# Two-stage attention and two feed-forward layers on one core: a transfer, the maxima, the weighted sums and the last results reordered

## The chip, the cores and the metric

The kernel runs on one core of a Trainium2 chip. The metric is the device time of one execution in microseconds (us). The engines are TensorE (PE, its weight loads PEld), VectorE (DVE), ScalarE (ACT), GpSimd (POOL) and SyncE (SP), which issues all the DMAs. Each engine takes its instructions in the order in which the program writes them.

## The reference, cut to what matters

```python
def sm_attn(qq, kk, vv):
    s = scale * np.matmul(qq, kk.transpose(0, 1, 3, 2))
    s = s - np.max(s, axis=-1, keepdims=True)
    a = np.exp(s)
    a = a / (np.sum(a, axis=-1, keepdims=True) + 1e-09)
    return np.matmul(a, vv)
p_packed = sm_attn(p, k, v)
out = sm_attn(q, p_packed, p_packed)      # 4 batches, 8 heads, 576 rows, 64 columns
x = out with its heads side by side       # 2304 x 512
x = softplus(x @ w_in) @ w_out            # 512 -> 2048 -> 512, in float32
return silu(x @ w_in2) @ w_out2
```

## The kernel before, in words

The schedule is written out by hand: the order in which the program emits instructions is each engine's order. A piece of work is a Python generator (`Item`) that yields the name of the point at which its next part is due. `run_steps` walks through 128 steps; `go(point)` runs the parts of the step's items that are due at that point. A step `s` goes: "next", "D0", "A0"; `emit_in(s)`, six matmuls that make one 128x288 block `h` of the hidden layer; "PE"; `emit_out(s)`, the matmuls of an output block `y` (in step 2 it stands ahead of `emit_in`); `act_scalar`, the softplus; "A1", "D1", "A2"; `act_vector`, the low part of the softplus; "D" and `finish_out`, which adds `y` to the sum `ya` (in steps 4 to 7 it stands ahead of "D"); then the step's loads. A point beginning with D holds VectorE work, with A ScalarE work, and "PE" TensorE work.

For batch `b`, with t = 8b, the items are:

- `att1(b)` packs the values: `scores` (L324, into two tiles of PSUM), maxima `top` (L330, L331, VectorE), `exp` (L337), transposes `turn` (L346), copies `turned` (L350, L353, ScalarE), weighted sums `weigh` (L361, 80 small matmuls), normalising (L386 to L389, VectorE), a transpose (L394) and its copy `pt` (L398). For b > 1 its parts stand in steps t-10, t-9, t-7, t-6 and t-5, so the scores of batch 2 are in step 6 and those of batch 3 in step 14.
- `att2(2b)` and `att2(2b+1)` are the second attention for 288 columns each: scores (L409, one PSUM tile), a transpose on VectorE (L418), maximum, subtraction (L420, L421), exponential (L423, ScalarE), then at point D0 sum, reciprocal, product and transpose (L425 to L430), and the split into `ax` (L435 ScalarE, L437 VectorE), which `emit_in` (L488) reads.
- `packed(b, qs)` multiplies the packed values with two chunks of the first weight (L454, one PSUM tile), copies the high part `vw` on ScalarE (L462) and subtracts for the low part on VectorE (L466, which reads the PSUM tile again). `packed(b, (0,))` stands in step 8b-4 and `packed(b, (1,))` in step 8b-3, that is 5, 13 and 21.

All of these tiles come from `two_banks()`, a pool with two buffers (`psa`), each of two PSUM banks. Four more banks hold `h` and `y`.

Weights come as 64-bit numbers. A chunk is loaded (L128), scaled on ScalarE (L140) and put together on VectorE (L152, L159); some are then split into high and low parts (L171, L173). `start()` writes out by hand what precedes the steps: loads, dummy matmuls `warm(n)` (L680, 2n instructions), batch 0's attention, and the conversion of the weight chunks ("i", 0 to 3) and ("o", 0 to 3) among it.

In `second()` the second layer is made by a Strassen-like scheme. At its end `group_of` makes, for each of the sums Q1, Q4, Q5, Q6, Q7, Q3, Q2 and for two halves d, a block on TensorE (L1008); `add_group` adds it on VectorE (L1023) and joins sums on GpSimd (`gps`, L1024) and VectorE (`vec`), and `send` (L1029) issues the transfer of a finished 128x384 block on SP's queue.

Of the kernel before, what the change touches and what calls it, by code (L numbers as in the profile page):

```python
# [13 lines left out]
ALU = mybir.AluOpType  # L14
# [4 lines left out]
B, H, S, D = 4, 8, 576, 64  # L19
# [7 lines left out]
KC = 5  # L27
# [23 lines left out]
def body(ctx, tc, kT, vv, qT, pT, wi1, wo1, wi2, wo2, out):  # L51
# [259 lines left out]
    def att1(b):  # L311

        HS = S // 2
        sm = l0.tile([P, 8], F32, name="sm", bufs=2)
        e, et, s1 = [None] * NR, [None] * NR, [None] * NR

        def scores():
            pz, kt = kts[b]
            s1[:] = two_banks(), two_banks()
            for half in range(2):  # L320
                for k in range(NK):
                    for r in range(NR):
                        rows = slice(64 * r, 64 * r + 64)
                        nc.tensor.matmul(  # L324
                            s1[r][32 * k:32 * k + 32, half, :HS], lhsT=pz[rows, k, :],
                            rhs=kt[rows, k, half * HS:(half + 1) * HS], start=True, stop=True,
                        )

        def top(r):
            nc.vector.tensor_reduce(out=sm[:, r:r + 1], in_=s1[r][:, :, :HS], axis=AX.XY, op=ALU.max)  # L330
            nc.vector.tensor_scalar(  # L331
                out=sm[:, 2 + r:3 + r], in0=sm[:, r:r + 1], scalar1=-SCALE, scalar2=None, op0=ALU.mult
            )

        def exp(r):
            e[r] = att.tile([P, S], F32, name=f"e{r}")
            nc.scalar.activation(  # L337
                out=e[r].rearrange("p (h s) -> p h s", h=2), in_=s1[r][:, :, :HS],
                func=AF.Exp, scale=SCALE, bias=sm[:, 2 + r:3 + r],
            )  # L340

        def turn(r):
            t = s1[r] = two_banks()
            for c in range(KC):
                n = min(P, S - c * P)
                nc.tensor.transpose(t[:n, c // 4, (c % 4) * P:(c % 4 + 1) * P], e[r][:, c * P:c * P + n], ident)  # L346

        def turned(r):
            et[r] = att.tile([P, KC, P], F32, name="et", bufs=2)
            nc.scalar.activation(  # L350
                out=et[r][:, :4, :], in_=s1[r][:, 0, :].rearrange("p (c f) -> p c f", c=4), func=AF.Copy
            )
            nc.scalar.activation(out=et[r][:64, 4, :], in_=s1[r][:64, 1, :P], func=AF.Copy)  # L353

        def weigh(r):
            vt = vts[b]
            for c in range(KC):
                n = min(P, S - c * P)
                for k in range(NK):
                    h = 2 * k + r  # L360
                    nc.tensor.matmul(  # L361
                        po[32 * k:32 * k + 32, r, :D1], lhsT=et[r][:n, c, 32 * k:32 * k + 32],
                        rhs=vt[:n, c, h * D1:(h + 1) * D1], start=(c == 0), stop=(c == KC - 1),
                    )

        yield "PE"
        scores()
        yield "D"
        top(0)
        top(1)  # L370
        yield "A1"
        exp(0)
        exp(1)
        yield "PE"
        turn(0)
        turn(1)
        yield "A1"
        turned(0)
        turned(1)
        yield "PE"  # L380

        po = two_banks()
        weigh(0)
        weigh(1)
        yield "D"
        nc.vector.tensor_scalar(out=sm[:, 4:6], in0=po[:, :, D], scalar1=1e-9, scalar2=None, op0=ALU.add)  # L386
        nc.vector.reciprocal(out=sm[:, 6:8], in_=sm[:, 4:6])
        px = att.tile([P, NR, D], F32, name="px")
        nc.vector.tensor_tensor(  # L389
            out=px, in0=po[:, :, :D], in1=sm[:, 6:8].unsqueeze(2).to_broadcast([P, NR, D]), op=ALU.mult  # L390
        )
        yield "PE"
        pt_ps = two_banks()[:, 0, :P]
        nc.tensor.transpose(pt_ps, px.rearrange("p r d -> p (r d)"), ident)  # L394
        yield "A1"

        pt = pts[b] = l0.tile([P, P], F32, name="pt", bufs=B)
        nc.scalar.activation(out=pt, in_=pt_ps, func=AF.Copy)  # L398
# [46 lines left out]
    def packed(b, qs):  # L445
        yield "PE"
        t = two_banks()
        wide = len(qs) > 1
        for k in range(NK):
            w = whl["i", 2 * qs[0] + (k if wide else k // 2)]  # L450
            w = w if wide else w[:, (k % 2) * 256:(k % 2 + 1) * 256]
            for r in range(NR):
                rows = slice(64 * r, 64 * r + 64)
                nc.tensor.matmul(  # L454
                    t[32 * k:32 * k + 32, r, :512 if wide else 256], lhsT=pts[b][rows, k * NP:(k + 1) * NP],
                    rhs=w[rows, :], start=True, stop=True,
                )
        yield "A1"
        vs = []
        for i, q in enumerate(qs):  # L460
            v = l0.tile([P, 2, NR, 256], F32R, name="vw", bufs=3)
            nc.scalar.activation(out=v[:, 0], in_=t[:, :, 256 * i:256 * i + 256], func=AF.Copy)  # L462
            vs.append(v)
        yield "D"
        for i, (q, v) in enumerate(zip(qs, vs)):
            nc.vector.tensor_tensor(  # L466
                out=v[:, 1], in0=t[:, :, 256 * i:256 * i + 256], in1=v[:, 0].bitcast(F32), op=ALU.subtract
            )
            vw[b, q] = v
# [149 lines left out]
    def plan_all():  # L619
# [48 lines left out]
            last = b == B - 1  # L668
            plan(Item(att2(2 * b + 1, last)), (t - 3, t - 1, t) + (t + 1,) * last)
        for (b, qs), s in vstep.items():  # L670
            plan(Item(packed(b, qs)), (s,))

    POINTS = "D0", "A0", "PE", "A1", "D1", "A2", "D"

# [11 lines left out]
    def start():  # L686
        load_k(0)
        load_w("i", 0)
        load_w("i", 1)
        load_v(0)  # L690
        load_q(0)
        load_w("o", 0)
        load_w("o", 1)
        a1 = [Item(att1(b)) for b in range(2)]
        a2 = [Item(att2(blk)) for blk in range(2)]
        v = Item(packed(0, (0,)))
        w = {(k, n): Item(conv_w(k, n, True)) for k in "io" for n in range(GJ)}
        warm(12)
        a1[0].run("PE")
        load_q(1)  # L700
        load_k(1)
        for n in 2, 3:
            load_w("i", n)
        for n in 2, 3:
            load_w("o", n)
        w["i", 0].run("A0", "D1")
        a1[0].run("D")
        w["i", 1].run("A0")
        a1[0].run("A1")
        w["i", 1].run("D1")  # L710
        warm(10)
        a1[0].run("PE", "A1", "D", "PE")
        load_v(1)
        warm(4)
        w["o", 0].run("A0")
        a1[0].run("D")
        w["o", 0].run("D1")
        a1[0].run("PE", "A1")
        a2[0].run("PE")
        v.run("PE")  # L720
        warm(14)
        a2[0].run("D1", "D")
        v.run("A1", "D")
        w["o", 1].run("A0")
        a2[0].run("A1")
        a2[1].run("PE")
        warm(8)
        a2[0].run("D0")
        a2[1].run("D1")
        a1[1].run("PE")  # L730
        a2[0].run("A1", "D")
        w["i", 2].run("A0")
        w["i", 3].run("A0")
        a2[1].run("D")
        w["o", 2].run("A0")
        a2[1].run("A1")
        w["o", 3].run("A0")
        a1[1].run("D", "A1")
        w["o", 1].run("D1")
        a2[1].run("D0")  # L740
        for item, s in (a2[1], 1), (Item(warm_item(10)), 1), (a1[1], 1), (a1[1], 2), (a1[1], 3):
            plan(item, (s,))
        for k, n, ss in ("i", 2, (1,)), ("i", 3, (2,)), ("o", 2, (3,)), ("o", 3, (4,)):
            plan(w[k, n], ss)

        OS = (3, 4), (4, 5), (5, 6), (10, 11)
        for n in range(GJ):
            plan(w["o", n], OS[n])

    def run_steps(end):  # L750
        for s in range(end):
# [14 lines left out]
            h = emit_in(s)  # L766
            go("PE")
            ys = emit_out(s) if ys is None else ys
            r = act_scalar(s, h)
            go("A1")  # L770
            go("D1")
# [8 lines left out]
                finish_out(s, *y)  # L780
            if late:
                go("D")
            for f in loads.get(s, ()):
                f()

# [144 lines left out]
    def second():  # L930
# [88 lines left out]
        def add_group(p, n, y):  # L1019
# [39 lines left out]
            if q == Q1:  # L1059
                gps(a[Q6], a[Q6], a[Q1])  # L1060
                gps(a[Q2], a[Q2], a[Q1])
            elif q == Q6:
                gps(a[Q5], a[Q5], a[Q6])
                gps(a[Q4], a[Q6], a[Q4], ALU.subtract)
            elif q == Q7:
                vec(a[Q4], a[q], a[Q4])
                send(1, 0, a[Q4])
                vec(a[q], a[q], a[Q5])
                send(1, 1, a[q])
            elif q == Q3:  # L1070
                gps(a[q], a[q], a[Q5])
                send(0, 1, a[q])
            elif q == Q2:
                send(0, 0, place(0, 0))

# [325 lines left out]
```

## Time and profile before

| | before |
|---|---|
| median of 3 runs | 743.41 us (743.38 to 743.85) |
| profiled execution, its own time | 744.61 us |
| its span, first to last instruction | 742.8 us |
| PE busy | 730.9 us (98%) |
| DVE busy | 563.7 us (76%) |
| ACT busy | 389.2 us (52%) |
| POOL busy | 161.7 us (22%) |

Busy is the time in which an engine had an instruction of its own running; matmuls are pipelined, so a busy PE also holds matmuls that wait behind each other. Times in rows are us from the start of the span. In a timeline row come the start, the length, the engine and line, the operation, what it writes and reads, the shape, the count of merged instructions, and, in brackets, how long the engine was idle before it and what ended that.

### The profile page before, as it was taken

The numbers are of one execution on the slowest core, as the hardware profiler recorded it, in microseconds if no ns is written. First come the engines' busy times: TensorE is split into PE (matmuls) and PEld (weight loads), VectorE is DVE, ScalarE is ACT, GpSimd is POOL, SyncE is SP. The second block draws the span as 40 slices with busy tenths as digits, with TensorE's granted clock in tenths as the row PEclk, the third lists the DMA queues.
The fourth block names the chain that finished last, engine by engine and source line by source line (L and its number), as shares of the span: only waits on it lengthen the run. The fifth ranks groups of instructions, "written<-read, shape, count | busy, mean of one in ns | idle before, by whom it ended". The sixth has DMA issues, their size and how long they took to land.

```text
span 742.8 us, 13862 instructions
## 1 busy us (share of the span) xinstructions
PE 730.9 (98%) x5404; PEld 697.9 (94%) x5404; DVE 563.7 (76%) x1020; ACT 389.2 (52%) x745; POOL 161.7 (22%) x138
## 2 busy tenths in 40 slices
PE   7999999999999999999999999999999999999997
PEld 6777889999999999999999999999999999999996
DVE  3888887879968897897746685767776976867666
ACT  3667876666555665566535544343354553454340
POOL 0000000000000000000000000000267999876656
PEclk9999999999999999999999999999999999999999
DMA  9965033144463362464349787889999789998932
GB/s 339 347 226 169 19 143 115 57 185 147 162 231 133 150 218 99 169 255 172 155 145 379 297 325 249 333 309 348 358 349 382 269 266 376 343 344 280 310 118 86
DMA packets 64674, 173.73 MB, mean 234 GB/s; under 512 B 5728, under 2 KB 34400, under 8 KB 61280
## 3 DMA queue, kind: packets, MB, share of 16 engines
q1 hardware_dynamic: 64608, 172.85, 65.2%
q8 instruction: 42, 0.69, 0.4%
q14 instruction: 24, 0.20, 0.1%
HBM read 136.65 MB, written 36.18 MB: 233 GB/s over the span
## 4 chain that ended last, share of the span: by engine, by line
PE 82%; DVE 6%; DMA 5%; ACT 4%; issue 1%; SPq 1%; POOL 0%; POOLq 0%; DVEq 0%
PE y L528 25%; PE h L488 13%; PE y L1008 11%; PE y L1112 8%; PE pA L950 6%; PE pB L950 6%; PE pC L950 6%; PE pD L950 3%; PE psa L454 2%; DMA wd<-whl 2%; DMA raw<-wi 2%; DMA wraw<-wo 2%; PE y L521 1%; DVE ya L1023 1%; PE psa L361 1%
## 5 line engine op out<-in xcount | busy, mean ns | idle before, releaser
L528 PE MATMUL y<-gh,w 128*128 128x288 f32 x960 | 212.1, 296 | 0.2 <-DVE ya L543 0.2
L528 PEld LDWEIGHTS y<-gh,w 128*128 128x128 f32 x960 | 160.4, 188 | 13.0 <-issue 5.5
L528 PE MATMUL y<-gl,w 128*128 128x288 f32 x480 | 141.8, 295 | 0.0
L982 POOL TENSOR_TENSOR sums<-c 128x384 f32<-128x384 f32 x13 | 15.6, 1199 | 551.4 <-ACT c L1264 551.4
L488 PE MATMUL h<-ax,vw 128*128 128x288 f32 x768 | 125.2, 298 | 0.8 <-DVE ax L437 0.7
L488 PEld LDWEIGHTS h<-ax,vw 128*128 128x128 f32 x768 | 109.3, 188 | 3.2 <-DVE ax L437 1.2
L1008 PE MATMUL y<-G,w 128*128 128x384 f32 x480 | 93.9, 334 | 0.0
L528 PEld LDWEIGHTS y<-gl,w 128*128 128x128 f32 x480 | 90.2, 188 | 0.5 <-DVE gl L505 0.5
L1112 PE MATMUL y<-G,w 128*128 128x384 f32 x480 | 89.5, 334 | 0.0
L500 ACT ACTIVATE gt<-h 128x288 f32<-128x288 f32 x120 | 48.6, 405 | 68.6 <-PE h L488 64.0
L1008 PEld LDWEIGHTS y<-G,w 128*128 128x128 f32 x480 | 84.1, 188 | 0.2 <-DVE ya L1023 0.2
L1112 PEld LDWEIGHTS y<-G,w 128*128 128x128 f32 x480 | 83.8, 188 | 0.0
L505 DVE TENSOR_TENSOR gl<-gt,gh 128x288 fp32r<-128x288 f32 x120 | 54.2, 451 | 25.2 <-ACT gh L501 24.3
L950 PE MATMUL pA<-xc,w 128*128 128x384 f32 x288 | 57.8, 334 | 0.1
L950 PE MATMUL pB<-xc,w 128*128 128x384 f32 x288 | 57.7, 334 | 0.0
L950 PE MATMUL pC<-xc,w 128*128 128x384 f32 x288 | 57.6, 334 | 0.0
L501 ACT ACTIVATE gh<-gt 128x288 fp32r<-128x288 f32 x120 | 53.4, 445 | 3.8
L545 DVE TENSOR_TENSOR ya<-y,ya 128x288 f32<-128x288 f32 x104 | 46.8, 451 | 7.2 <-PE y L528 7.0
L950 PEld LDWEIGHTS pA<-xc,w 128*128 128x128 f32 x288 | 50.4, 188 | 0.4 <-ACT ta L1182 0.4
L950 PEld LDWEIGHTS pB<-xc,w 128*128 128x128 f32 x288 | 50.6, 188 | 0.0
L1260 ACT ACTIVATE tc<-tc 128x384 f32<-128x384 f32 x24 | 12.6, 526 | 72.4 <-DVE tc L1160 72.3
L990 POOL TENSOR_TENSOR G<-sums,G 128x384 fp32r<-128x384 f32 x40 | 49.0, 1248 | 7.1 <-ACT G L986 7.1
(143 smaller groups left out, 1167.7 us busy)
## 6 DMA issues: line engine op xcount, KB each, us to landing
w<-wd SPq DMA_DIRECT2D x84, 512.0 KB, 6.0
wd<-whl SPq DMA_DIRECT2D x8, 1792.0 KB, 7.1
w<-td SPq DMA_DIRECT2D x56, 256.0 KB, 6.4
w<-od SPq DMA_DIRECT2D x42, 256.0 KB, 5.8
w<-od SPq DMA_DIRECT2D x20, 512.0 KB, 6.6
wraw<-wi SPq DMA_DIRECT2D x16, 512.0 KB, 5.5
wraw<-wo SPq DMA_DIRECT2D x16, 512.0 KB, 6.2
raw<-wi SPq DMA_DIRECT2D x16, 512.0 KB, 6.0
```

Of the source, the lines that this page charges most:

```text
L454: nc.tensor.matmul(t[32 * k:32 * k + 32, r, :512 if wide else 256], lhsT=pts[b][rows, k * NP:(k + 1) * NP], rhs=w[rows, :], start=True, st ...
L488: nc.tensor.matmul(h, lhsT=w, rhs=x, start=(i == 0), stop=(i == len(mm) - 1))
L500: nc.scalar.activation(out=gt, in_=h, func=AF.Softplus)
L501: nc.scalar.activation(out=gh, in_=gt, func=AF.Copy)
L505: nc.vector.tensor_tensor(out=gl, in0=gt, in1=gh.bitcast(F32), op=ALU.subtract)
L528: nc.tensor.matmul(y, lhsT=w[:, c], rhs=g, start=(j == js[0] and m == 0), stop=(j == js[-1] and m == 2))
L545: nc.vector.tensor_tensor(out=acc, in0=y, in1=acc, op=ALU.add)
L950: nc.tensor.matmul(out, lhsT=a, rhs=b, start=start and not i, stop=not start and i == len(mm) - 1, skip_group_check=True,)
L982: eng.tensor_tensor(out=sum_of(q), in0=a, in1=b, op=op)
L990: eng.tensor_tensor(out=u[:, 1], in0=sum_of(q), in1=u[:, 0].bitcast(F32), op=ALU.subtract)
L1008: nc.tensor.matmul(y, lhsT=w, rhs=g, start=not m, stop=m == len(mm) - 1)
L1112: nc.tensor.matmul(y, lhsT=a[:, c], rhs=G[:, g, h, j], start=(k % 2 == j == m == 0), stop=(k % 2 == j == 1 and m == 2),)
```

## The change

It moves work; no operation is added or dropped.

1. In `start()`, the load of the values (`load_v(0)`) is issued ahead of that of weight chunk ("i", 1). VectorE does the maxima of batch 0 ahead of putting chunk ("i", 0) together; scaling and putting together ("i", 1) move behind the weighted sums; putting together ("o", 0) moves far back, to stand beside that of ("o", 1); ("o", 0) and ("o", 1) are scaled later. Batch 0's transpose (L394) now stands ahead of `warm(4)`.
2. In the steps, `weigh` gets a point "PE2" behind `emit_out` and its normalising a point "D2" at the step's end, behind `finish_out`. For b > 0 the chunks of 128 rows of both heads' halves come ahead of the two chunks of 64 rows.
3. For b > 0, `packed(b, (1,))` leaves its VectorE subtraction (L466) to point "D1" of the following step.
4. At the end of `second()`, GpSimd makes Q4 ahead of Q5; the two VectorE operations and two sends of a half (`second_row`) are put off: those of d = 0 behind the addition of Q7's other half, those of d = 1 behind Q3's results.

```diff
-        def weigh(r):
+        def weigh(*at):
             vt = vts[b]
-            for c in range(KC):
+            for r, c in at:
...
-        yield "PE"
+        yield "PE2"
 
         po = two_banks()
-        weigh(0)
-        weigh(1)
-        yield "D"
+        chunks = [(r, c) for r in range(NR) for c in range(KC)]
+        weigh(*(sorted(chunks, key=lambda rc: rc[1] == KC - 1) if b else chunks))
+        yield "D2"
...
-        yield "D"
+        if b and qs == (1,):
+            yield "next"
+            yield "D1"
+        else:
+            yield "D"
         for i, (q, v) in enumerate(zip(qs, vs)):
...
         for (b, qs), s in vstep.items():
-            plan(Item(packed(b, qs)), (s,))
+            plan(Item(packed(b, qs)), (s, s + 1) if b and qs == (1,) else (s,))
...
         load_w("i", 0)
+        load_v(0)
         load_w("i", 1)
-        load_v(0)
...
-        w["i", 0].run("A0", "D1")
+        w["i", 0].run("A0")
         a1[0].run("D")
+        w["i", 0].run("D1")
+        a1[0].run("A1")
+        warm(10)
+        a1[0].run("PE", "A1", "PE2")
         w["i", 1].run("A0")
-        a1[0].run("A1")
-        w["i", 1].run("D1")
-        warm(10)
-        a1[0].run("PE", "A1", "D", "PE")
+        a1[0].run("D2", "PE")
         load_v(1)
         warm(4)
-        w["o", 0].run("A0")
-        a1[0].run("D")
-        w["o", 0].run("D1")
-        a1[0].run("PE", "A1")
+        w["i", 1].run("D1")
+        a1[0].run("A1")
         a2[0].run("PE")
         v.run("PE")
         warm(14)
         a2[0].run("D1", "D")
         v.run("A1", "D")
+        w["o", 0].run("A0")
+        a2[0].run("A1")
         w["o", 1].run("A0")
-        a2[0].run("A1")
         a2[1].run("PE")
...
         a1[1].run("D", "A1")
+        w["o", 0].run("D1")
         w["o", 1].run("D1")
         a2[1].run("D0")
...
             ys = emit_out(s) if ys is None else ys
+            go("PE2")
...
             if late:
                 go("D")
+            go("D2")
             for f in loads.get(s, ()):
...
             elif q == Q6:
+                gps(a[Q4], a[Q6], a[Q4], ALU.subtract)
                 gps(a[Q5], a[Q5], a[Q6])
-                gps(a[Q4], a[Q6], a[Q4], ALU.subtract)
             elif q == Q7:
-                vec(a[Q4], a[q], a[Q4])
-                send(1, 0, a[Q4])
-                vec(a[q], a[q], a[Q5])
-                send(1, 1, a[q])
+                def second_row():
+                    vec(a[Q4], a[q], a[Q4])
+                    send(1, 0, a[Q4])
+                    vec(a[q], a[q], a[Q5])
+                    send(1, 1, a[q])
+                todo.append(second_row)
+                if d:
+                    todo.pop(0)()
             elif q == Q3:
                 gps(a[q], a[q], a[Q5])
                 send(0, 1, a[q])
+                if d:
+                    todo.pop(0)()
```

## Rows read from the trace of the kernel before

**Rows 1.** The page, busy time, share of the span and instructions of each engine.
```profile
PE 730.9 (98%) x5404; PEld 697.9 (94%) x5404; DVE 563.7 (76%) x1020; ACT 389.2 (52%) x745; POOL 161.7 (22%) x138
```

**Rows 2.** Waits of PE in the whole span: us in total, times, longest us.
```profile
PE psa L361 <- ACT et L353: 1.0, 2, 0.6
PE h L488 <- DVE ax L437: 0.7, 2, 0.5
```

**Rows 3.** Timeline of the start, 0 to 45 us.
```profile
6.73 1.17 PE L324 MATMUL psa<-kt,pz 64*32 64x288 f32 x24 [0.23 <-DMA kt<-kT]
...
10.03 0.75 DVE L330 TENSOR_REDUCE sm<-psa 128x1 f32<-128x576 f32 x1
...
26.21 0.68 ACT L140 ACTIVATE wraw<-wraw 128x512 f32<-128x512 f32 x1 [0.46 <-DMA wraw<-wo]
...
26.85 0.69 ACT L423 ACTIVATE tr<-tr 128x576 f32<-128x576 f32 x1
...
28.44 0.42 DVE L152 TENSOR_SCALAR wx<-wraw 128x512 int32<-128x512 int32 x1
...
29.50 0.75 DVE L425 TENSOR_REDUCE mx<-tr 128x18 f32<-128x576 f32 x1
...
34.12 0.80 PE L488 MATMUL h<-ax,vw 128*128 128x288 f32 x4 [0.46 <-DVE ax L437]
```

**Rows 4.** One stretch: us, busy PE, PEld, DVE, ACT, POOL, PEclk, DMA share, GB/s.
```profile
20.00:30.00 10.00, 10.00 (x114) 8.30 (x113) 9.49 (x18) 6.32 (x10) 0.00 (x0) 1.00 1.03 397
```

**Rows 5.** Timeline around steps 5 and 6.
```profile
47.12 0.68 ACT L423 ACTIVATE tr<-tr 128x576 f32<-128x576 f32 x1
...
48.36 0.68 DVE L466 TENSOR_TENSOR vw<-psa,vw 128x512 fp32r<-128x512 f32 x1
...
49.27 1.20 PE L324 MATMUL psa<-kt,pz 64*32 64x288 f32 x32
...
51.65 0.78 DVE L430 STREAM_TRANSPOSE tb<-tr 128x576 f32<-128x576 f32 x1
```

**Rows 6.** Timeline around steps 13 and 14.
```profile
74.04 0.69 DVE L466 TENSOR_TENSOR vw<-psa,vw 128x512 fp32r<-128x512 f32 x1
74.27 1.71 PE L324 MATMUL psa<-kt,pz 64*32 64x288 f32 x32
...
76.72 0.78 DVE L430 STREAM_TRANSPOSE tb<-tr 128x576 f32<-128x576 f32 x1
```

**Rows 7.** Timeline around steps 18 and 19.
```profile
90.99 0.15 DVE L386 TENSOR_SCALAR sm<-psa 128x2 f32<-128x2 f32 x1
...
91.59 0.45 DVE L543 COPY ya<-y 128x288 f32<-128x288 f32 x1
...
92.02 0.27 PE L394 MATMUL psa<-ident,px 128*128 128x128 f32 x1
```

**Rows 8.** Timeline of the end.
```profile
731.96 1.35 DVE L1023 TENSOR_TENSOR ya<-ya 128x384 f32<-128x384 f32 x1 [1.18 <-POOL ya L1024]
...
733.34 6.88 SPq L1029 DMA_DIRECT2D yT<-ya  x8
...
735.18 0.56 DVE L1023 TENSOR_TENSOR ya<-ya 128x384 f32<-128x384 f32 x1
...
736.25 1.94 DVE L1023 TENSOR_TENSOR ya<-y,ya 128x384 f32<-128x384 f32 x4
...
736.94 1.96 POOL L1024 TENSOR_TENSOR ya<-ya,acc 128x384 f32<-128x384 f32 x2 [2.75 <-DVE ya L1023]
```

**Rows 9.** The last two stretches, with the columns of rows 4.
```profile
730.00:737.50 7.50, 7.50 (x43) 7.02 (x41) 6.15 (x10) 0.00 (x0) 4.75 (x5) 1.00 0.26 93
737.50:742.80 5.30, 0.01 (x1) 0.00 (x0) 0.69 (x2) 0.00 (x0) 1.40 (x2) 0.92 0.47 168
```

**Rows 10.** Timeline of the start, the dummy matmuls.
```profile
1.36 4.52 PE L680 MATMUL y<-ident 128*128 128x128 f32 x24 [1.36 <-POOL ident masks.py:199]
...
7.83 2.50 PE L680 MATMUL y<-ident 128*128 128x128 f32 x20
```

## The prediction

> **What bounds the kernel now.** The page comes first: TensorE is busy for 730.9 us, 98% of the span [rows 1]. So time can be won or lost only where TensorE stands still or runs dummy work: ahead of the first real matmuls, at its few waits, and behind its last matmul. The table of its waits gives two that this change aims at: the weighted sums wait twice for ScalarE's copies, 1.0 us in all, and `emit_in` waits twice for VectorE's low part of `ax`, 0.7 us in all [rows 2]. One of the latter is the 0.46 us at 34.12 [rows 3], so the other is some 0.2 us. Then I read the timeline of the start, of steps 5, 6, 13 and 14, of steps 18 and 19, and of the end. The measure I use is TensorE's order: from 34 us on, a delay of TensorE is a delay of the whole kernel unless a later wait takes it up.
>
> **The start.** The maxima can begin when the scores end, 6.73 + 1.17 = 7.90, where they now begin at 10.03 [rows 3]: the chain of batch 0 comes up to 2.1 us earlier. What follows does not keep it. ScalarE's order still has the scaling of chunk ("o", 2) ahead of the exponential of block 1. That scaling waits for its transfer until 26.21, and the exponential starts at 26.85, directly behind it [rows 3]. The transfer cannot land sooner: the DMA engines are at a share of 1.03 in this stretch [rows 4], and the change swaps two loads without taking a byte away. So the exponential stays where it is and ends at 27.54. Behind it VectorE's sum (L425, now 29.50) is set by what stands ahead of it on VectorE, and there the change adds the putting together of ("o", 0), as long as that of the one there now, 29.50 - 28.44 = 1.06 us [rows 3]. If the chain on VectorE comes 1.3 us earlier (less than 2.1, because the scaling of chunk ("i", 0) still precedes the exponentials and `warm(4)` now follows the transpose), the sum comes 1.3 - 1.06, about 0.3 us, earlier, and so does the matmul at 34.12. I take -0.3 us. The ends are 0 and -1.0 (all 2.1 less the 1.06). The cover that keeps this small is ScalarE's wait for the transfer. SyncE's own order has the values' two loads one place earlier and the chunk's behind them; with the engines full this changes which lands first and no later landing.
>
> **The weighted sums behind `emit_out`.** The longer of the two waits, 0.6 us in step 18 [rows 2], goes, for `emit_out` now fills it. What is late next is the normalising: it starts at 90.99 and is done when the add of the step starts at 91.59, and the transpose on TensorE follows at 92.02 [rows 7]. VectorE was at work on other things until 90.99, so the sums were not what it waited for. The change puts the normalising behind that add, 0.45 us [rows 7], and puts only `emit_in` between the sums and the transpose. The normalised values then come at about 91.59 + 0.45 = 92.04, the transpose some 0.1 us later: within 0.1 us of now. The wait moves from ahead of the sums to ahead of the transpose. I take the same for batch 2 and so 0 for the part; its ends are -1.0 (both waits of rows 2 vanish) and +0.5 (the add's length, on a VectorE with nothing else late). Sorting the chunks changes no count of matmuls, and what it could win is the wait already counted.
>
> **The subtraction left to the next step.** This part decides. `att1(b+1)` takes both buffers of the pool for its scores; one of them is the tile that L466 reads. In step 14 the scores begin at 74.27 and take 1.71 us, where the same 32 matmuls take 1.20 in step 6 [rows 5, 6]. The 0.5 us more is the time until L466 ends, 74.04 + 0.69 = 74.73: the second score matmul waits until the subtraction has left the bank. In step 6 L466 ends at 49.04 and the scores begin at 49.27, just past it [rows 5]. After the change L466 stands, for batches 1 and 2, in "D1" of steps 6 and 14, the very steps whose "PE" holds these scores, and behind the step's "D0", which is L425 to L430. Those run on VectorE right behind L466 now, and with it moved they run first: the exponential that they read ends at 47.80 [rows 5], so nothing holds them. As only the order changes, L466 ends about where L430 ends now. Step 6: 51.65 + 0.78 = 52.43, and TensorE, which starts the scores at 49.27, goes on at 52.45: **+3.2 us**. Step 14: 76.72 + 0.78 = 77.50, less 0.1 us of idle time that VectorE had ahead of L466, against the 74.73 of now: **+2.7 us**. TensorE takes instructions in order, so `emit_out`, the next `emit_in` and with them ScalarE's softplus all queue behind the scores. The ends of each are 2.0 (if ScalarE's work done meanwhile takes up a wait later) and 3.4 (L466's whole move, 52.43 - 49.04).
>
> For batch 3 no scores follow. There the D0 part comes 0.7 us earlier (the length of L466), and the second wait of `emit_in`, about 0.2 us, goes: -0.2 us.
>
> **What a stall does to the clock.** The granted clock is 1.00, the level of 2.4 GHz, where TensorE works [rows 4, 9]; it averages 0.92 in the last 5.3 us alone, when TensorE has nothing more to do [rows 9]. No row shows it lower between two matmuls, so I add nothing to the stalls. The Trainium skill, "TensorE: Matmul & The Clock Gate", section "HAM oscillation — how this bites in real kernels", speaks against the change here: a pause of TensorE for data can put it back to half rate, and each pause pays again for the way back. By it the sum would be that of the third rival below; by the row it is the one here.
>
> **The end.** Now VectorE waits 1.18 us at 731.96 for GpSimd before it can make the second row, and its additions of Q3 and Q2 all come after, from 736.25. GpSimd's two joins of Q3 wait 2.75 us for them and end at 738.90, and SyncE's eight issues end at 740.22, Q2's behind Q3's [rows 8]. After the change VectorE, free from 731.96 - 1.18 = 730.78, adds Q7's second half when TensorE has made it: 36 matmuls follow it (6 for each half of Q3, 12 for each of Q2), at 7.50 / 43 = 0.174 us each [rows 9], which puts it 6.3 us ahead of 737.5, at 731.2. It makes the d = 0 row by 734.2 (two operations of 1.35, the length beside a busy GpSimd, where 0.56 is that beside an idle one [rows 8], and its place in line), adds both halves of Q3 by 735.1, and the d = 1 row by 737.2 (one of 1.35, one between 0.56 and 1.35). GpSimd makes Q3's joins, 1 us each, by 736.8, beside it. Q2's two additions take half of 1.94 us and end at about 738.1, just past TensorE's end at 737.5 [rows 9]. The last issue then starts at about 738.45; now it starts near 739.85 (the last issue of the 6.88 us, 0.38 long): -1.4 us. The ends are -1.9 (the last addition directly behind TensorE) and -0.8 (both operations of the last row at 1.35 and the sends one behind another).
>
> **Sum.** -0.3 + 0 + 3.2 + 2.7 - 0.2 - 1.4 = +4.0 us. The profiled execution took 744.61 us (1.8 around its span of 742.8), which becomes 748.6. The median of the runs lies 1.2 below the profiled one, 743.41, so I forecast 747.4 us. A measurement can tell about 0.2%, 1.5 us, from no change.
>
> **Rivals.**
>
> 1. *No wait for the bank (faster).* Place: the second score matmul of steps 6 and 14. If the program gives the scores banks that need not wait for the moved subtraction, both stalls drop out and the sum is -1.9: 741.5 us. It decides if the scores start within 0.2 us of `emit_in`'s end. For it: no row shows a tile read behind the allocation of its successor. Against it: step 14 shows the wait as it is, and two buffers leave no third. Chance 0.12.
> 2. *More given back (slower, but less).* The start keeps -1.0, and both waits of the weighted sums, 1.0 us, go since ScalarE and VectorE catch up during the stalls: 4.0 - 0.7 - 1.0 = +2.3, 745.7 us. Against it: in the rows ScalarE's softplus waits on TensorE's `h`, so it is delayed with it. Chance 0.16.
> 3. *The clock falls in the stalls.* The first 24 dummy matmuls, behind 1.36 us of idling, took 4.52 us, 188 ns each, against 125 ns (2.50 for 20) later [rows 10]: 24 x 63 ns = 1.5 us for a slow beginning. Once gives 748.9, twice 750.4 us. Chance 0.06.
>
> That the change does not do what it says holds for two parts in the forecast itself: the start's transfer and the weighted sums win next to nothing there.
>
> **Numbers.** The forecast has 0.66: its own range is 746.0 to 748.8. The rivals have 0.12, 0.16 and 0.06. The range of 744.6 to 749.4 holds the forecast with its bounds, nearly all of the second rival and half of the third, and leaves out the first. Slower by over 0.2% (above 744.9): 0.66 + 0.14 + 0.06, less a little for gains that add up, 0.83. Faster 0.12, and 0.05 between.
>
> **What would show it.** Right: in steps 6 and 14 the scores (L324) stretch from 1.2 to over 4 us, or TensorE idles behind DVE `vw` L466; L466 follows L430; the exponential near 26.85 does not move; a wait stands ahead of L394 in place of that ahead of L361; the last issue starts some 1.4 us sooner after TensorE's last matmul. Wrong: scores of 1.2 us right behind `emit_in` in both steps make the change a gain; a granted clock under 1.00 between 45 and 90 us makes it dearer.

## The result and the profile after

| | before | after |
|---|---|---|
| median (6 runs each, same chip) | 743.58 us | 750.14 us (749.25 to 751.11) |
| ratio | | 1.0086, 95% interval 1.0073 to 1.0099 |
| profiled execution, its own time | 744.61 us | 751.11 us |
| its span | 742.8 us | 749.3 us |
| span ahead of TensorE's last matmul / behind it | 737.5 / 5.3 us | 744.7 / 4.6 us |

The kernel got slower, as forecast, but by 6.6 us where the forecast said 4.0, and the time lies above the range (744.6 to 749.4). Of the runs below, one execution of weigh_only (888.56 us) and one of scale_late (1019.19 us) ran at a mean granted clock of 0.75 and 0.66 and count in no ratio; the former is weigh_only's profiled one, so that part is read in the trace of sub_early.

The page's first part and the table of TensorE's waits, after (against [rows 1, 2]):

```profile
PE 733.4 (98%) x5404; PEld 700.2 (93%) x5404; DVE 564.1 (75%) x1020; ACT 389.2 (52%) x745; POOL 162.3 (22%) x138
```
```profile
PE psa L324 <- DVE vw L470: 4.9, 2, 2.5
PE psa L394 <- DVE px L389: 1.8, 2, 0.9
...
PE psa L361 <- ACT et L353: 0.2, 1, 0.2
```

At the top stands a wait that was not in the table before: the score matmuls (L324) for the subtraction of `vw` (L470, which was L466). The wait of the weighted sums (L361) has shrunk to 0.2 us, that of `emit_in` for `ax` is no longer in the table, and one ahead of the transpose L394 has come (one of its two, 0.9 us, lies in the start, beside dummy work). But the waits for the subtraction come to 4.9 us, less than the 6.6 us, and TensorE is busy for 2.5 us *more* with the same 5404 matmuls. The timeline of TensorE around steps 5 to 7 and 13 to 15, after (against [rows 5, 6]):

```profile
48.04 1.18 PE L492 MATMUL h<-ax,vw 128*128 128x288 f32 x6
...
49.15 0.67 PE L324 MATMUL psa<-kt,pz 64*32 64x288 f32 x2
...
52.33 2.17 PE L324 MATMUL psa<-kt,pz 64*32 64x288 f32 x30 [2.51 <-DVE vw L470]
...
56.67 1.18 PE L492 MATMUL h<-ax,vw 128*128 128x288 f32 x6
...
77.76 0.96 PE L492 MATMUL h<-ax,vw 128*128 128x288 f32 x6
78.65 0.67 PE L324 MATMUL psa<-kt,pz 64*32 64x288 f32 x2
81.73 1.38 PE L324 MATMUL psa<-kt,pz 64*32 64x288 f32 x30 [2.41 <-DVE vw L470]
...
86.07 0.96 PE L492 MATMUL h<-ax,vw 128*128 128x288 f32 x6
```

Two score matmuls run, the other thirty wait, as forecast. From one `emit_in` to the next, step 6 takes 56.67 - 48.04 = 8.63 us and step 14 takes 86.07 - 77.76 = 8.31. Before, the same distances were:

```profile
48.16 1.18 PE L488 MATMUL h<-ax,vw 128*128 128x288 f32 x6
...
52.23 1.18 PE L488 MATMUL h<-ax,vw 128*128 128x288 f32 x6
...
73.38 0.96 PE L488 MATMUL h<-ax,vw 128*128 128x288 f32 x6
...
77.60 0.96 PE L488 MATMUL h<-ax,vw 128*128 128x288 f32 x6
```

that is 4.07 and 4.22 us. So the two steps lose 4.56 and 4.09 us, not 3.2 and 2.7. The rest lies behind the waits: in step 6 thirty scores take 2.17 us where all 32 took 1.20 [rows 5]. The stretches by windows, after (columns of rows 4):

```profile
40.00:51.90 11.90, 9.82 (x102) 6.71 (x100) 10.57 (x18) 8.48 (x16) 0.00 (x0) 1.00 0.52 184
51.90:55.31 3.41, 2.98 (x32) 1.40 (x33) 0.37 (x1) 0.52 (x1) 0.00 (x0) 0.50 0.02 5
55.31:82.60 27.29, 24.45 (x290) 19.15 (x289) 23.38 (x48) 19.13 (x35) 0.00 (x0) 1.00 0.50 170
82.60:86.03 3.43, 3.43 (x26) 2.99 (x13) 1.84 (x5) 0.00 (x0) 0.00 (x0) 0.50 0.00 0
86.03:740.00 653.97, 652.57 (x4481) 636.78 (x4480) 498.00 (x896) 340.61 (x656) 157.42 (x129) 1.00 0.65 232
```

The granted clock is 0.50 (1.2 GHz) in two stretches of 3.4 us, and 1.00 (2.4 GHz) in the others. The first stretch begins in the wait of step 6, 0.43 us before the scores go on at 52.33; the second begins at 82.60, 0.87 us after they went on at 81.73. Matmuls that run at the lower level count as busy, so what the clock costs shows as more "work" and not as a wait.

### The profile page after: what moved, and what is told of

It is laid out like the page before. It is cut to its first block, busy times and chain, and to the rows that moved or that the text cites. A ratio compares the mean times of both kernels' runs of the same rounds, so it can differ in the third digit from the quotient of the medians.

```text
span 749.3 us, 13862 instructions
## 1 busy us (share of the span) xinstructions
PE 733.4 (98%) x5404; PEld 700.2 (93%) x5404; DVE 564.1 (75%) x1020; ACT 389.2 (52%) x745; POOL 162.3 (22%) x138
## 4 chain that ended last, share of the span: by engine, by line
PE 87%; DVE 4%; ACT 3%; DMA 3%; issue 1%; SPq 1%; DVEq 0%; ACTq 0%
PE y L532 25%; PE h L492 12%; PE y L1015 12%; PE y L1125 11%; PE pA L957 7%; PE pB L957 7%; PE pC L957 7%; PE pD L957 3%; DMA wraw<-wo 3%; PE psa L454 2%; PE y L525 1%; DVE ya L1030 1%; ACT e L337 1%; PE psa L324 0%; PE psa L409 0%
```

## The experiments

All medians in us; "before" is the kernel before, run beside it on the same chip.

| run | median | before | ratio (95% interval) |
|---|---|---|---|
| sub_early | 742.80 | 743.83 | 0.9989 (0.9980 to 0.9997) |
| sub_late_only | 750.64 | 743.83 | 1.0095 (1.0080 to 1.0111) |
| warm_in_wait | 747.70 | 743.83 | 1.0055 (1.0042 to 1.0068) |
| sub_late_b3 | 742.06 | 743.83 | 0.9979 (0.9970 to 0.9988) |
| weigh_only | 743.61 | 743.78 | 0.9996 (0.9987 to 1.0005) |
| end_only | 742.66 | 743.78 | 0.9984 (0.9975 to 0.9992) |
| start_only | 743.88 | 743.78 | 1.0003 (0.9994 to 1.0012) |
| turn_later | 742.59 | 743.78 | 0.9988 (0.9977 to 0.9998) |
| scale_late | 743.83 | 743.73 | 1.0000 (0.9991 to 1.0009) |
| sub_late_b1 | 748.30 | 743.73 | 1.0056 (1.0042 to 1.0069) |
| best | 740.46 | 743.73 | 0.9956 (0.9944 to 0.9969) |

### The subtraction put back, and alone

**sub_early**: the changed kernel without its third part.

```diff
-        if b and qs == (1,):
+        if False:
...
-            plan(Item(packed(b, qs)), (s, s + 1) if b and qs == (1,) else (s,))
+            plan(Item(packed(b, qs)), (s,))
```

> The changed kernel with one part undone: the subtraction L470 of the packed chunk (b, 1) is back at the end of its own step. Theory (the score matmuls of steps 6 and 14 wait for that subtraction, and the clock falls after each wait): both waits and both half-clock stretches go, 4.5 us at step 6 and 4.1 at step 14 as the two traces show them; back come the 0.4 to 0.7 us that the later subtraction gave back between steps 16 and 27. So about 742.2 us, between 741.5 and 743.0, with a granted clock of 1.00 from 8 us to the end. Rival (the weighted sums behind the output product, or the new start, cost the time): still above 747 us. Rival (the waits cost only their own length and the clock fell for another reason): the clock still shows 0.50 somewhere between 45 and 90 us.

Measured 742.80: the loss is gone, and the other three parts together are a small gain. The recorded clock is 1.00 from 6 us until past TensorE's last matmul.

**sub_late_only**: the kernel before with the third part alone (the same lines of the diff as in the change).

> The kernel before with that one part alone: the subtraction L466 of the packed chunk (b, 1) in the next step, for batches 1 to 3. Theory: the whole loss is here, 4.5 + 4.1 us less 0.5 to 0.8 us for the wait ahead of the output product and the one for the low part of ax that go: 743.5 + 7.9 = 751.4 us, between 750 and 752, with two waits of PE psa L324 on DVE vw of 2.4 to 2.9 us and a granted clock of 0.50 behind each. Rival (the deferral alone is harmless and the loss needs the other moves): within 1.5 us of 743.5.

Measured 750.64, 6.8 us above the kernel before, 0.8 below the middle of what was expected. Its profile shows both waits, 2.51 and 2.38 us, but the clock falls behind the second alone:

```profile
52.54 1.20 PE L324 MATMUL psa<-kt,pz 64*32 64x288 f32 x30 [2.51 <-DVE vw L470]
```
```profile
49.00:54.00 5.00, 2.49 (x37) 1.11 (x36) 3.34 (x7) 2.45 (x4) 0.00 (x0) 1.00 0.04 10
...
82.10:85.50 3.40, 3.40 (x17) 3.40 (x16) 1.95 (x5) 0.00 (x0) 0.00 (x0) 0.50 0.00 0
```

So its step 6 has the wait without the clock: from `emit_in` at 48.25 to the next at 55.49 it takes 7.24 us, 3.17 more than before. The whole loss comes from this part; its size depends on whether the clock follows.

### The wait and the clock told apart

**warm_in_wait**: dummy matmuls keep TensorE at work while the scores cannot go on.

```diff
+                plan(Item(warm_item(10)), (t - 10,))
                 plan(Item(att1(b)), (t - 10, t - 9, t - 7, t - 6, t - 5))
```

> The changed kernel with ten dummy matmuls (20 instructions) ahead of the scores in steps 6 and 14, so that TensorE works through most of each wait; the subtraction stays late. Theory (the wait is set by VectorE alone and a second price is the clock that falls when TensorE stands still): the scores go on at the same distance from the start of the step, the granted clock stays 1.00, and the time falls by the price of the clock, 2 x 1.4 us: 750.1 - 2.8 = 747.3 us. Rival (the matmuls behind the wait are slow for a reason that is not the clock): no change, 750 us, or more, as the dummy matmuls add to TensorE's queue.

The timeline of TensorE in steps 6 and 14 of this run:

```profile
47.80 1.18 PE L492 MATMUL h<-ax,vw 128*128 128x288 f32 x6
48.82 2.39 PE L685 MATMUL y<-ident 128*128 128x128 f32 x20
51.14 0.67 PE L324 MATMUL psa<-kt,pz 64*32 64x288 f32 x2
52.09 1.20 PE L324 MATMUL psa<-kt,pz 64*32 64x288 f32 x30 [0.28 <-DVE vw L470]
...
55.05 1.18 PE L492 MATMUL h<-ax,vw 128*128 128x288 f32 x6
...
76.11 0.96 PE L492 MATMUL h<-ax,vw 128*128 128x288 f32 x6
...
82.93 0.96 PE L492 MATMUL h<-ax,vw 128*128 128x288 f32 x6
```

Adding twenty instructions ahead of each wait makes the kernel 2.4 us faster than the change (2.7 when each is taken against the kernel before that ran beside it). The scores go on 4.29 us after the step's `emit_in` began (52.09 - 47.80), just as without the dummies (52.33 - 48.04): VectorE sets the wait. The thirty scores are back at 1.20 us, and the clock is 1.00 through both steps:

```profile
48.90:55.00 6.10, 5.82 (x60) 4.18 (x59) 3.46 (x7) 2.12 (x3) 0.00 (x0) 1.00 0.12 22
76.50:84.00 7.50, 7.29 (x77) 6.00 (x76) 6.58 (x14) 3.48 (x7) 0.00 (x0) 1.00 0.17 67
```

So the wait by itself is 55.05 - 47.80 - 4.07 = 3.18 us in step 6 and 82.93 - 76.11 - 4.22 = 2.60 us in step 14, and the clock is the rest of the 4.56 and 4.09: 1.4 and 1.5 us. Step 6 of sub_late_only, without dummies and at 1.00, gave 3.17 for the same wait. The 2.9 us of clock are those of the profiled execution, the slowest of the change's six; the medians differ by 2.4 to 2.7.

**sub_late_b1**: the kernel before with the later subtraction for batch 1 alone, so with one wait.

```diff
-        yield "D"
+        if b == 1 and qs == (1,):
+            yield "next"
+            yield "D1"
+        else:
+            yield "D"
...
-            plan(Item(packed(b, qs)), (s,))
+            plan(Item(packed(b, qs)), (s, s + 1) if b == 1 and qs == (1,) else (s,))
```

> The kernel before with the later subtraction for batch 1 alone, so with one wait, in step 6. Theory: the wait costs 3.2 us and the clock, where it falls, 1.4 us more. With the 0.4 us wait ahead of the weighted sums of batch 2 still there: 747.0 us where the clock holds, 748.4 where it falls, so the runs spread over more than a microsecond. Rival (the two waits cost only together): within 1.5 us of 743.8.

Its five runs fall apart by their mean clock: 747.08 and 747.39 at 0.999, 748.30 and 748.59 at 0.997, 750.56 at 0.995. The first two are 3.4 to 3.7 us above the kernel before, the price of the wait; the next two 1.2 us more, one fall of the clock. The profiled one is the slowest, by windows:

```profile
49.00:52.10 3.10, 1.20 (x7) 0.50 (x5) 2.96 (x7) 1.95 (x3) 0.00 (x0) 1.00 0.08 24
52.10:58.90 6.80, 6.18 (x39) 3.60 (x40) 1.02 (x2) 0.69 (x1) 0.00 (x0) 0.50 0.43 145
58.90:62.00 3.10, 3.10 (x18) 2.69 (x17) 2.87 (x7) 2.10 (x3) 0.00 (x0) 1.00 0.17 68
```

The same program, with the same wait of 2.5 us, ran at half rate for 6.8 us, twice as long as in the change. The wait's cost is fixed by the program; what the clock adds is 0, 1.2 or some 3 us from run to run. The runs of the change, at mean clocks of 0.994 to 0.997, spread over 1.9 us, which fits the same cause, though their times do not follow their mean clocks strictly. What decides how long the clock stays down, no run here shows.

**sub_late_b3**: the changed kernel with the later subtraction for batch 3 alone.

```diff
-        if b and qs == (1,):
+        if b == B - 1 and qs == (1,):
...
-            plan(Item(packed(b, qs)), (s, s + 1) if b and qs == (1,) else (s,))
+            plan(Item(packed(b, qs)), (s, s + 1) if b == B - 1 and qs == (1,) else (s,))
```

> The changed kernel with the later subtraction kept for batch 3 alone, where no scores follow in the next step. Theory: as the kernel with the subtraction undone, less the wait of emit_in for the low part of ax in step 24, about 0.3 us: 741.9 us against 742.2. Rival (the later subtraction is no gain anywhere): equal to the undone one within 0.2 us.

Measured 742.06, 0.74 below sub_early. Moving the subtraction is a gain where no scores follow, and a larger one than the wait in the table. From `emit_in` of step 24 to that of step 27 sub_early takes 8.08 us, as the kernel before, and sub_late_b3 7.49: 0.6 us of the gain lies there, where the table of waits has 0.26. In sub_early that `emit_in` is

```profile
105.53 0.53 PE L492 MATMUL h<-ax,vw 128*128 128x288 f32 x2
...
106.33 0.80 PE L492 MATMUL h<-ax,vw 128*128 128x288 f32 x4 [0.26 <-DVE ax L437]
```

Two of the six matmuls had started and count as busy while the other four waited: they begin 0.80 us after the first two.

### The other parts alone

**weigh_only**: the kernel before with the second part alone.

> The kernel before with the weighted sums behind the output product, the normalising at the step's end and the sorted chunks alone. Theory (the wait only moves, from ahead of the sums to ahead of the transpose): the waits of psa L361 on ScalarE, 0.4 and 0.6 us, vanish, a wait of psa L394 on VectorE of about 0.9 us appears in step 19, and the sum over steps 9 to 20 is between 0 and +0.3 us: 743.8 us. Rival (the moved sums win what the waits cost): -1.0 us, 742.6.

Measured 743.61, no difference from the kernel before. Where the wait went is seen in sub_early, which holds the same part: its timeline around step 18 and 19 (against [rows 7]).

```profile
88.15 1.48 PE L361 MATMUL psa<-vt,et 128*32 128x65 f32 x80
89.56 1.06 PE L492 MATMUL h<-ax,vw 128*128 128x288 f32 x6
...
91.51 0.30 PE L394 MATMUL psa<-ident,px 128*128 128x128 f32 x1 [0.89 <-DVE px L389]
```
and in the changed kernel VectorE's part of the same chain:
```profile
99.46 0.45 DVE L547 COPY ya<-y 128x288 f32<-128x288 f32 x1
99.82 0.15 DVE L386 TENSOR_SCALAR sm<-psa 128x2 f32<-128x2 f32 x1
...
100.21 0.29 DVE L389 TENSOR_TENSOR px<-psa,sm 128x128 f32<-128x128 f32 x1
100.64 0.30 PE L394 MATMUL psa<-ident,px 128*128 128x128 f32 x1 [0.89 <-DVE px L389]
```

The normalising follows the step's add and the transpose follows the normalising, after a wait of 0.89 us: the wait has changed its place.

**turn_later**: sub_late_b3 with the transpose behind `emit_out`.

```diff
-        yield "PE"
+        yield "PE2"
         pt_ps = two_banks()[:, 0, :P]
...
-        a1[0].run("D2", "PE")
+        a1[0].run("D2", "PE2")
```

> The changed kernel with the later subtraction for batch 3 alone, and the transpose of the packed values (L394) moved behind emit_out of its step, so that it does not stand ahead of the output product while VectorE normalises. Theory (the moved wait ahead of L394 costs some 1.2 us in step 19): that wait goes and the time falls by 0.8 to 1.2 us against the kernel with the transpose where it was, 742.06: about 741.0 us. Rival (the copy of the transposed values then comes late and the next scores L409 wait in its place): no gain, 742 us.

Measured 742.59, 1.2 us below its kernel before, where sub_late_b3 was 1.8 below: the expected gain did not come. The wait ahead of L394 in step 19 is gone, but the table of waits has a new one at its top:

```profile
PE h L492 <- DVE vw L470: 1.6, 1, 1.6
```

It lies in step 4, at 41.6 us. In step 3 the transpose of batch 1 stands beside the first `packed(0, (1,))`, whose `vw` the next `emit_in` needs at once. The copy `pt`, which now waits for the later transpose until 40.01, stands ahead of the copy of `vw` on ScalarE, which starts at 40.19. Against sub_late_b3, TensorE's order by the traces wins 0.3 us for batch 2 and 1.1 for batch 3 and loses 1.9 between the `emit_in` of step 3 and that of step 4. The run "best" below leaves batch 1 out.

**end_only**: the kernel before with the fourth part alone.

> The kernel before with the reordered end alone. Theory by the traces (the stretch from TensorE's last matmul to the end of the span shrinks from 5.33 to 4.55 us and the bank wait of 0.17 us goes): -0.9 us, 742.7. Rival (my forecast's -1.4 us, if part of it lies ahead of TensorE's last matmul): 742.2.

Measured 742.66, 1.1 us below the kernel before. The stretch behind TensorE's last matmul shrinks, from 5.33 us to 4.66 in this run's trace; the bank wait that was to go is still there (0.16 us), and some 0.4 us of the difference of medians is not placed. The end of the changed kernel, which has the same order (against [rows 8]):

```profile
741.84 2.30 POOL L1031 TENSOR_TENSOR ya<-ya,acc 128x384 f32<-128x384 f32 x2
741.87 1.40 DVE L1030 TENSOR_TENSOR ya<-ya 128x384 f32<-128x384 f32 x1
743.38 1.18 DVE L1030 TENSOR_TENSOR ya<-ya,acc 128x384 f32<-128x384 f32 x1
744.48 1.01 DVE L1030 TENSOR_TENSOR ya<-y,ya 128x384 f32<-128x384 f32 x2
744.60 2.10 SPq L1036 DMA_DIRECT2D yT<-ya  x4
```

GpSimd's two joins of Q3 and VectorE's second row run side by side and hold each other up: 1.40 and 1.18 us on VectorE where 0.56 is the length alone, and 2.30 for GpSimd's two where they took 1.96 [rows 8]. Behind VectorE's last addition, which ends at 745.49, SyncE still has sends in its queue: the last four follow one another from 744.60 to 746.70, so the last one starts near 746.31, 1.57 us behind TensorE's last matmul (744.74). Before, it started 2.34 us behind it.

**start_only**: the kernel before with the first part alone.

> The kernel before with the reordered start alone. Theory (ScalarE's scaling of the third and fourth output chunk waits for transfers and holds the exponentials): the first emit_in comes over 1 us earlier, the third between 0.1 and 0.7 us earlier, so 743.2 us, between 742.8 and 743.7. Rival (the values' earlier transfer carries through): -1.3 us, 742.3.

Measured 743.88, no difference, and outside what was expected. In the trace the first `emit_in` comes 1.4 us earlier (24.28 against 25.70), the third not at all (33.25 against 33.13), and the fourth 0.4 us earlier (36.16 against 36.53). That is no more than one run differs from the next: with an unchanged start (end_only) the fourth stands at 35.97, and the 0.46 us wait of the third for `ax` [rows 3] is absent there too.

**scale_late**: the scaling of chunks ("o", 2) and ("o", 3) behind the exponentials, in start_only.

```diff
-        w["o", 2].run("A0")
         a2[1].run("A1")
-        w["o", 3].run("A0")
         a1[1].run("D", "A1")
+        w["o", 2].run("A0")
+        w["o", 3].run("A0")
```

> The reordered start alone, and in it the scaling of the output chunks 2 and 3 moved behind the exponentials on ScalarE. Theory (ScalarE's scaling, held by its transfer, is one cover and VectorE's queue a second one behind it): the exponential L423 now near 27.6 comes over 1 us earlier, the first output product near 32.1 comes up to 1 us earlier, but the third emit_in still waits for the low part of ax near 33.9, so the time moves by less than 0.4 us against the start alone: 743.6 us. Rival (the transfer's wait was the only cover): -1.0 us, 742.9.

Measured 743.83: the theory's "no gain", but not by all of its steps. ScalarE's timeline in this run, and the row of VectorE's sum:

```profile
25.96 0.67 ACT L140 ACTIVATE wraw<-wraw 128x512 f32<-128x512 f32 x1 [1.32 <-DMA wraw<-wi]
26.53 0.67 ACT L423 ACTIVATE tr<-tr 128x576 f32<-128x576 f32 x1
27.10 1.35 ACT L337 ACTIVATE e<-psa,sm 128x576 f32<-128x576 f32 x2
28.35 1.25 ACT L140 ACTIVATE wraw<-wraw 128x512 f32<-128x512 f32 x2
29.62 1.28 ACT L494 ACT_TABLE_LOAD   x1
```
```profile
29.12 0.74 DVE L425 TENSOR_REDUCE mx<-tr 128x18 f32<-128x576 f32 x1
```

The exponential stands only 0.5 us earlier than in start_only (26.53 against 27.02): with the third chunk out of the way it is the chunk before it, ("i", 3), whose transfer lands late. And the softplus still stands behind all the scalings, so the first output product does not move (31.37 against 31.42). VectorE's sum behind the exponential does not move either (29.12 against 29.15 in start_only): VectorE puts two chunks together from 26.99 on, one instruction behind the other, and comes to the sum after them. So there is not one cover but a row of them, and VectorE's queue, the theory's second cover, is one in which no wait for a transfer is listed.

### A version that beats both

**best**: the changed kernel with the later subtraction for batch 3 alone, the transpose behind `emit_out` for batches 2 and 3, the scalings as in scale_late, and the putting together of chunk ("i", 2) one step later.

```diff
-        yield "PE"
+        yield "PE2" if b > 1 else "PE"
...
-        for k, n, ss in ("i", 2, (1,)), ("i", 3, (2,)), ("o", 2, (3,)), ("o", 3, (4,)):
+        for k, n, ss in ("i", 2, (2,)), ("i", 3, (2,)), ("o", 2, (3,)), ("o", 3, (4,)):
```

> The changed kernel with the later subtraction for batch 3 alone, the transpose of the packed values behind emit_out for batches 2 and 3, the scaling of the output chunks 2 and 3 behind the exponentials, and the putting together of weight chunk (i, 2) one step later. Theory: against 742.06 with the first of these alone, the wait ahead of L394 in step 19 goes (-1.0 us) and VectorE reaches the low part of ax some 0.7 us earlier in the start: 740.4 us, between 739.8 and 741.2. Rival (the start is bound by the transfers themselves): 741.1, the transpose alone.

Measured 740.46 us, 3.3 us below the kernel before and as expected, but not by the expected parts: in the traces it is 0.1 us ahead of sub_late_b3 at step 6, so the start gives next to nothing, and another 1.3 us by step 23, the transposes' share. With the later subtraction confined to the batch that has no scores behind it, the transpose moved in turn wins its wait: in step 19 it stands without one at 91.60 (in sub_early it had waited 0.89 us).

## Why the prediction was right and where it was wrong

- **The step that failed** is "No row shows it lower between two matmuls, so I add nothing to the stalls." The trace of before had no stall of TensorE as long as those the change makes (the longest in its table is 1.5 us), so its rows could not show what one does; I took the absence for a zero. The change's profile shows 0.50 with both waits, and warm_in_wait prices it: 1.4 + 1.5 = 2.9 us in that execution, 2.4 to 2.7 by the medians, and the forecast missed by 2.7 (747.4 against 750.14). The third rival had the mechanism and a size near it: 750.4 us where the clock falls twice. I gave it 0.06. That it comes so close is partly luck: its 1.5 us was read from the start's dummy matmuls, and the gains of the forecast, -1.9 in all, are about right only because their errors cancel (below). The rule of the Trainium skill quoted there ("TensorE: Matmul & The Clock Gate", section "HAM oscillation — how this bites in real kernels"), that a pause for data can put TensorE back to half rate, agrees with the change's trace, 0.50 with both waits; in sub_late_only the first wait left the clock at 1.00.
- **The two waits** were right in place and size: forecast 3.2 and 2.7 us, measured 3.18 and 2.60 with the clock held by dummies, and 3.17 for the first without them. The argument that two swapped pieces of VectorE's order end where the last of them ended needed no other number. That the whole change turns on this part is shown by sub_early and sub_late_only.
- **The batch without scores**: forecast -0.2, measured -0.74 (sub_late_b3 against sub_early). The term came from the table of waits, which counts only the time in which no started matmul was in flight.
- **The weighted sums**: forecast 0, measured 0 (743.61 against 743.78). The wait moved to the transpose as forecast; it is dearer there (0.89 us against 0.60), and the sorted sums take 0.27 us less in each batch (see the last section). The forecast had said that sorting could win nothing but the wait, so its 0 is right by two errors that cancel.
- **The start**: forecast -0.3 with 0 as one end, measured no difference that can be told. ScalarE does hold the exponential by a scaling that waits for its transfer, but that this is the cover that keeps the gain small does not hold: in scale_late that scaling is out of the way, the exponential comes 0.5 us earlier than in start_only, and VectorE's sum stays where its own queue puts it, as the forecast also said.
- **The end**: forecast -1.4 with -0.8 as one end, measured -1.1 (end_only). By the traces the last issue starts 0.77 us sooner behind TensorE's last matmul, not 1.4. The mis-sized term is the sends: the forecast had the last one start 0.35 us after VectorE's last addition, and it starts 0.82 after it, behind three others in SyncE's queue, as the -0.8 end had it. VectorE's last row is dearer than forecast (1.40 and 1.18 us), but the row before it was cheaper (0.71 and 1.19 where I took two of 1.35), and its last addition ends 0.75 us behind TensorE where the forecast said 0.6.
- The second rival, that ScalarE and VectorE catch up in the stalls and give back 1.7 us, is not seen: between steps 15 and 27 the change gives back some 0.6 us in all, most of it by the later subtraction of batch 3.

## What to carry to other kernels

Before a read of a buffer is put off, list who takes the buffer next in program order: with as many tiles in use as the pool has, the reader's new place, not the writer's, sets when the next user starts, and on an in-order engine everything behind that user. A stall of TensorE should be priced twice, by its length and by half-rate matmuls behind it; dummy matmuls placed in a wait separate the two, and buy back the second. A wait that is filled by reordering is won only if the next waiter's producer was not the late one: ask what the moved work's consumer will wait for before counting the gain.

## What was not expected of the hardware

- The same wait of 2.5 us left the clock at 1.00 in one run (step 6 of sub_late_only), put it to 0.50 for 3.4 us in another (the change) and for 6.8 us in a third (sub_late_b1). A kernel with such a wait has no single time: one program took 747.1, 748.3 and 750.6 us.
- The eighty small matmuls of the weighted sums take 1.48 us when the blocks of 64 rows come last, and 1.75 when they stand between blocks of 128 rows, the same in eight traces: batch 0, which the change does not sort, keeps its 1.75 in the change too. The sorting saves 0.27 us of TensorE's time in each of batches 1 to 3. The row of the order before, in step 18:

```profile
87.85 1.75 PE L361 MATMUL psa<-vt,et 128*32 128x65 f32 x80 [0.60 <-ACT et L353]
```
